# A start ordered by hand up to the guard's branch, and the softmax sums' load two steps earlier

## The chip, the core and the metric

The kernel runs on one core of one Trainium2 chip. The metric is the device time of one execution in microseconds; before the change the median of three runs is 1902.31 us (1900.91 to 1903.0). The engines are TensorE (matmuls and transposes), VectorE, ScalarE, GpSimd and SyncE (SP), which issues most transfers.

## The reference, cut to what matters

One layer norm feeds two branches, whose results are added to the input:

```python
xn = layernorm(x)                                   # x: 2048 x 512
# A: attention, 32 heads of 16, one shared key and value head
p  = softmax(einsum("bhqd,bkd->bhqk", q, k) * 16**-0.5)
A  = einsum("bhqk,bkd->bhqd", p, v) ... @ wo
# B: product-key experts, 4096 experts, per token and head 2 of 64 x 64
s1, s2 = q1 @ k1.T, q2 @ k2.T                       # top 2 of each, top 2 of the 4 sums
g  = softmax(top_s);  act = gelu(xn . u[top_e])
B  = sum(g * act * v[top_e])
return x + A + B
```

In the inputs B has 32 heads with two halves of 128, so its queries' product with the keys is folded into a weight of 512 columns for each chunk of four heads (8 chunks).

## The kernel before, in words

The 2048 rows are 16 tiles of 128, in four groups of four tiles. Numbers that must keep float32 precision are split in a high and a low part, and a product is the sum of three matmuls (high by high, high by low, low by high).

The start (L1213 to L1253) does the following for each group g: load x, norm_group (L145: statistics and normalisation on VectorE, one square root on ScalarE), transpose_group (L171: 16 transposes, a copy on ScalarE and a subtraction on VectorE for each of four 512-wide tiles, a store to DRAM for later groups), project_kv (L194: 12 matmuls for the shared key and value, the key's parts copied by six small transfers into kaug), and project_q (L222: four blocks r of 12 matmuls, a high part on ScalarE, a low part on VectorE, both stored to DRAM; the square of the block is summed by a matmul with blk, for the length of the queries). wq is split into halves first (L1227 to L1232).

The experts' part starts there too. score_thread (L1114) is a generator: wp_make(c) (L482) folds chunk c's weights with four products (pw, from a loaded tile wqT) and four sets of transposes (pwt) with splits; item (L519) then gives one tile's scores for the chunk (12 matmuls psc) and finds the best by max and max_index on VectorE; the fourth item of a chunk ends in batch (L569), which makes indices and gates. Each step yields a cost, which is added to a planned time, spent. run_scores (L1130) drives it to a planned time or to a key. In the start it runs chunk 0 to its end. The gathers (L987) then fetch expert rows by index into up to NGB = 12 buffers, which they share with other tiles of the start.

guard (L251) compares a bound, the longest query by the longest key, with a limit. The flag is loaded by all engines, and the rare branch computes true maxima; with these inputs it isn't taken. In front of this branch the order of the instructions is the framework's planner's. Behind it, an order written by hand holds: each engine's queue has the instructions in the order of the program text.

The loop (L1256 to L1347) has 256 steps d of att_steps (L1159), i = 2d. In a step four score pairs (sc: two 64-row matmuls) go to PSUM, ScalarE takes their exponentials (pt), and the value products (pv) of the step before follow. A unit u is 16 values of i: 512 queries and four heads. In the middle (mid) come VectorE's dots and sums for the gathered experts; at the end fill() runs run_scores up to a planned time, aim, which grows evenly with d. So TensorE is filled with chunk products, and in phases 2 and 3 with a dense form of the experts (dense, L655).

Two units make a pair pp. Its softmax sums go to DRAM at the start of the step with r = i mod 32 = 2 (unit_tail's spread, L351); pair_load (L372) reads them back as 128 x 32 at r = 4, pair_invert (L377) takes reciprocals on VectorE at r = 6 and stores them, pair_spread (L382) reads them broadcast at r = 10, and pair_tail (L387) multiplies. At the start of the step with r = 4, load_q (L308) issues eight transfers for the next unit; SP issues in order, and a transfer's wait blocks what is behind it.

At i = 0 the step loads the maxima rows of the query tile (load_q with rows=False) and runs two steps of wp_make(1) ahead of the first scores (L1167).

Of the kernel before, what the change touches and what calls it, by code (L numbers as in the profile page):

```python
# [11 lines left out]
F32 = mybir.dt.float32  # L12
# [43 lines left out]
def tile_kernel(ctx, tc, x, wq, wkv, wo, wqT, kT, uv, ub, vb, out):  # L56
# [39 lines left out]
    zk(kaug)  # L96
    qa_bufs = []
# [4 lines left out]
    vaug = const.tile([P, NT, 32], F32, name="vaug")  # L102
    nc.gpsimd.memset(vaug, 1.0)
# [15 lines left out]
    ones_f = start.tile([2, 512], F32, name="ones_f")  # L119
    nc.gpsimd.memset(ones_f, 1.0)  # L120
# [6 lines left out]
    XT, XS, XN, ACC, XP = [], {}, {}, {}, [None]  # L127
# [17 lines left out]
    def norm_group(g, xs):  # L145
        mv = start.tile([P, GT, 2], F32, name="mv", bufs=2)
        for j in range(GT):
            st = start.tile([P, 6], F32, name="st", bufs=2)
            nc.vector.bn_stats(st, xs[j])
            nc.vector.bn_aggr(mv[:, j, :], st)  # L150
        v = start.tile([P, GT], F32, name="ve", bufs=2)
        nc.vector.tensor_scalar(v, mv[:, :, 1], 1e-5, None, op0=OP.add)
        sd = start.tile([P, GT], F32, name="sd", bufs=2)
        nc.scalar.activation(sd, v, AF.Sqrt)
# [9 lines left out]
        for j in range(GT):  # L164
            t = g * GT + j
            nc.vector.tensor_scalar(XN[t], xs[j], mv[:, j, 0:1], rs[:, j:j + 1],
                                    op0=OP.subtract, op1=OP.mult)
            if 1 <= g < NSP:
                nc.sync.dma_start(d_xn[t - TPH], XN[t])

    def transpose_group(g):  # L171
        first = g < 1
        XS[g] = []
        for k in range(KC):
# [10 lines left out]
            XS[g].append(xt)  # L185
            if not first:
                nc.sync.dma_start(d_xt[g - 1][k], raw(xt[:]))
# [3 lines left out]
    ksq_p = None  # L191
    qmax = const.tile([P, NGRP], F32, name="qmax")

    def project_kv(g):  # L194
        p = stile("pkv")[:, 0, :]
        n = 0
        for k in range(KC):
            for a, b in TERMS:
                w = (wkv_h, wkv_l)[a]
                nc.tensor.matmul(p[:32, :], w[:, k, :], XS[g][k][:, b, :], start=n == 0, stop=n == 11)  # L200
                n += 1
        kv = big.tile([32, 512], F32, name="kv", tag="wk", bufs=NWK)
        nc.scalar.copy(kv, p[:32, :])
        kh = big.tile([32, 2, 512], F32R, name="kh", tag="wk", bufs=NWK)
        nc.vector.tensor_copy(kh[:, 0, :], kv)
        nc.vector.tensor_tensor(out=kh[:, 1, :], in0=kv, in1=kh[:, 0, :], op=OP.subtract)
        c = slice(g * 512, (g + 1) * 512)
        for base in (0, 64):
            nc.sync.dma_start(raw(kaug[base:base + 16, c]), raw(kh[:16, 0, :]))
            nc.sync.dma_start(raw(kaug[base + 16:base + 32, c]), raw(kh[:16, 1, :]))  # L210
            nc.sync.dma_start(raw(kaug[base + 32:base + 48, c]), raw(kh[:16, 0, :]))
        sq = start.tile([16, 512], BF16, name="ksq", tag="sq", bufs=2)
        nc.vector.tensor_mul(sq, kv[:16, :], kv[:16, :])
        nc.tensor.matmul(ksq_p[32 * g:32 * g + 32, :], blk[:16, 0:1].to_broadcast([16, 32]), sq,
                         start=True, stop=True)
# [6 lines left out]
    def project_q(g, wqs):  # L222
        pq = xtile("pqs")
        for r in range(KC):
            p = stile("pq")[:, 0, :]
            n = 0
            for k in range(KC):
                for a, b in TERMS:
                    nc.tensor.matmul(p, wqs[k][:, a, r * P:(r + 1) * P], XS[g][k][:, b, :],
                                     start=n == 0, stop=n == 11)  # L230
                    n += 1
            q = [start.tile([P, 512], F32R, name="qt", tag="qt", bufs=4) for _ in range(2)]
            nc.scalar.copy(q[0], p)
            nc.vector.tensor_tensor(out=q[1], in0=p, in1=q[0], op=OP.subtract)
            sq = start.tile([P, 512], BF16, name="qsq", tag="sq", bufs=2)
            nc.scalar.activation(sq, p, AF.Square)
            nc.tensor.matmul(pq[32 * r:32 * r + 32, :], blk, sq, start=True, stop=True)
            c = slice(g * 512, (g + 1) * 512)
            nc.sync.dma_start(d_qh[r * P:(r + 1) * P, c], raw(q[0][:]))
            nc.sync.dma_start(d_ql[r * P:(r + 1) * P, c], raw(q[1][:]))  # L240
        nc.vector.reduce_max(qmax[:, g:g + 1], pq, axis=AX.X)
# [9 lines left out]
    def guard():  # L251

        mm = small.tile([P, 2], F32, name="mm", bufs=1)
        nc.vector.reduce_max(mm[:, 0:1], qmax, axis=AX.X)
        nc.vector.reduce_max(mm[:, 1:2], ksq_p, axis=AX.X)
        p = xtile("pm")
        for i in range(2):
            nc.tensor.transpose(p[:1, i * P:(i + 1) * P], mm[:, i:i + 1], ident)
        m2 = small.tile([1, 2], F32, name="m2", bufs=1)
        nc.vector.reduce_max(m2, p[:1, :2 * P].rearrange("p (a n) -> p a n", a=2), axis=AX.X)  # L260
        pr = small.tile([1, 1], F32, name="prd", bufs=1)
        nc.vector.tensor_mul(pr, m2[:, 0:1], m2[:, 1:2])
        fl = small.tile([1, 1], I32, name="flag", bufs=1)
        nc.vector.tensor_scalar(fl, pr, LIMIT2, None, op0=OP.is_gt)
        flag = nc.values_load(fl[0:1, 0:1], min_val=0, max_val=1)
# [205 lines left out]
    def wp_load(c, h):  # L471
        if late[0] is None or (c == 1 and h < 2):
            w = gtile(F32, (P, 2, D), "wqt") if c == 0 and h > 1 else big.tile([P, 2, D], F32, name="wqt", tag="wqt", bufs=2)
        else:
            w = late[0].tile([P, 2, D], F32, name="wqt", tag="gy", bufs=3)
# [6 lines left out]
    def wp_make(c):  # L482
# [13 lines left out]
        for k in range(KC):  # L496
# [7 lines left out]
            store(lambda k=k, wk=wk: nc.sync.dma_start(d_w[c][:, k], raw(wk[:])))  # L504
# [570 lines left out]
    ON_ACT, LATER_ACT, LAST, LATER, BEHIND, STORES, POST, POST_FILL = [], [], [], [], [], [], [], []  # L1075
    store = STORES.append
# [81 lines left out]
    def att_steps(d, mid, fill):  # L1158
# [4 lines left out]
        if i < STEPS:  # L1163
            u, kc = divmod(i, 16)
            if i == 0:
                load_q(0, rows=False)
                run_scores(until=spent[0] + 1.8)  # L1167
# [20 lines left out]
        if pp and pp < 16:  # L1188
            if r == 4:
                pair_load(pp - 1)  # L1190
# [20 lines left out]
    xs = [[load_x(j, True) for j in range(GT)]]  # L1211
    wraws = []
    for i in range(2):  # L1213
        wraw = gtile(F32, (P, 2, 512))
        nc.sync.dma_start(wraw, wq[i * 256:(i + 1) * 256, :].rearrange("(k p) n -> p k n", p=P))
        wraws.append(wraw)
    for h in range(4):
        wp_load(0, h)
    for g in (1, 2):
        xs.append([load_x(g * GT + j, False) for j in range(GT)])  # L1220
    norm_group(0, xs[0])
    transpose_group(0)
    ksq_p = ps.tile([P, 512], F32, name="ksq_p", tag="pv", bufs=1)
    nc.vector.tensor_copy(wkv_h, wkv_f)
    nc.vector.tensor_tensor(out=wkv_l, in0=wkv_f, in1=wkv_h, op=OP.subtract)
    wqs = []
    for i in range(2):  # L1227
        for k in range(2):
            w = start.tile([P, 2, 512], F32R, name="wqs", tag="wqs", bufs=4)
            nc.scalar.copy(w[:, 0, :], wraws[i][:, k, :])  # L1230
            nc.vector.tensor_tensor(out=w[:, 1, :], in0=wraws[i][:, k, :], in1=w[:, 0, :], op=OP.subtract)
            wqs.append(w)  # L1232
    project_kv(0)
    norm_group(1, xs[1])
# [153 lines left out]
```

## Time and profile before

| what | us |
| --- | --- |
| runs, median | 1902.31 |
| profiled execution | 1899.53 |
| its span, first to last instruction | 1897.7 |
| TensorE busy | 1813.9 |
| VectorE busy | 1628.2 |
| ScalarE busy | 1286.8 |
| GpSimd busy | 694.7 |

The mean granted clock of TensorE is 0.991. A row of the timeline has the start, the length, the engine, the line, the operation with its output and inputs, and how many are merged; in brackets stands the idle time before it and what ended it. PEld is the weight load, which runs beside the matmul. A name with a q (SPq, PEq) is an engine's queue or sequencer. Matmuls are pipelined, and their ends in the trace are modelled.

### The profile page before, as it was taken

Reading aid. Unit: us, or ns where it says so; the run is one execution under the profiler, and the core shown is the slowest. Engines: PE = TensorE matmul, PEld = TensorE weight load, DVE = VectorE, ACT = ScalarE, POOL = GpSimd, SP = SyncE. Lnnn points to the kernel's source line nnn. Section 1 sums busy time; section 2 is a strip of 40 time slices with the busy share of each in tenths; the row PEclk is TensorE's granted clock in tenths of the full one; section 3 lists DMA queues with packets and bytes.
Section 4 is the critical chain, followed back from the end, with each engine's and each line's share of the span. In section 5 each row is a group of like instructions: output and inputs, shape, how many; then the busy total and the mean of one; then the engine's idle time right before and its main releaser. Section 6 shows DMA issues by size and latency. Waiting matters only on the chain.

```text
span 1897.7 us, 34925 instructions
## 1 busy us (share of the span) xinstructions
PE 1813.9 (96%) x10990; PEld 956.6 (50%) x10990; DVE 1628.2 (86%) x6381; ACT 1286.8 (68%) x1739; POOL 694.7 (37%) x920
## 2 busy tenths in 40 slices
PE   6979998999999899999999899999998999999998
PEld 3634444555555344555555454555544355555553
DVE  6628888999988977999899797999989778999995
ACT  3346665655557987887777555555579877788874
POOL 1203444434443123344434354344531124444430
PEclk9989999999999999999999999999999999999999
DMA  7857899897773677889899887877735868899883
GB/s 267 317 194 284 304 323 310 294 334 247 235 263 109 222 245 233 258 266 284 266 287 315 321 316 234 267 260 236 254 109 194 271 205 274 287 292 292 277 274 105
DMA packets 243706, 489.75 MB, mean 258 GB/s; under 512 B 93748, under 2 KB 106420, under 8 KB 243516
## 3 DMA queue, kind: packets, MB, share of 16 engines
q0 software_dynamic: 73728, 268.47, 42.4%
q1 hardware_dynamic: 168552, 218.18, 35.1%
q8 instruction: 88, 1.44, 0.3%
q10 hardware_dynamic: 1236, 0.82, 0.1%
q14 instruction: 102, 0.84, 0.1%
HBM read 426.49 MB, written 55.61 MB: 254 GB/s over the span
## 4 chain that ended last, share of the span: by engine, by line
PE 75%; DVE 9%; DMA 4%; ACT 3%; issue 2%; SPq 1%; DVEq 0%; ACTq 0%
PE pv L341 21%; PE psc L536 19%; PE sc L327 15%; PE pact L738 9%; PE pout L876 8%; DVE oh L797 2%; PE pwo L439 2%; ACT pt L330 2%; DVE xa L1043 1%; PE pw L492 1%; DVE g L1008 1%; DMA gy<-dg 1%; DVE oh L800 1%; DMA wqt<-in_wqT_dram 1%; DVE oh L799 1%
## 5 line engine op out<-in xcount | busy, mean ns | idle before, releaser
L330 ACT ACTIVATE pt<-sc 128x1024 f32<-128x1024 f32 x1024 | 994.5, 1028 | 433.8 <-PE sc L327 431.1
L996 POOL DMA_INDIRECT g<-in_uv_dram,idx x512 | 554.7, 1083 | 1013.8 <-DVE xa L1043 508.9
L341 PE MATMUL pv<-pt,vaug 128*32 128x512 f32 x4096 | 494.8, 601 | 0.0
L327 PE MATMUL sc<-qa,kaug 64*128 64x512 f32 x2048 | 387.7, 450 | 20.1 <-ACT pt L330 19.5
L536 PE MATMUL psc<-wk,xt 128*128 128x512 f32 x1536 | 388.2, 400 | 3.8 <-DVE wk L502 3.8
L1043 DVE SCALAR_TENSOR_TENSOR xa<-g,w,xa 128x512 f32<-128x512 f32 x512 | 371.1, 743 | 0.1
L1008 DVE CUSTOM_DVE_ANT_0 g<-g,xa 128x512 f32<-128x512 f32 x512 | 334.5, 679 | 9.5 <-DMA g<-in_uv_dram,idx 9.5
L536 PEld LDWEIGHTS psc<-wk,xt 128*128 128x128 f32 x1536 | 277.9, 188 | 107.1 <-issue 40.4
L327 PEld LDWEIGHTS sc<-qa,kaug 64*128 64x128 f32 x2048 | 156.8, 185 | 337.8 <-ACT pt L330 244.2
L341 PEld LDWEIGHTS pv<-pt,vaug 128*32 128x32 f32 x4096 | 107.1, 109 | 243.5 <-issue 243.5
L876 PE MATMUL pout<-wk,wd 128*128 128x512 f32 x768 | 197.3, 405 | 9.9 <-DVE wd L939 7.0
L551 DVE FIND_INDEX8 i<-m,psc 128x8 uint32<-128x64 f32 x1024 | 206.0, 218 | 0.0
L738 PE MATMUL pact<-xt,wk 128*128 128x512 f32 x768 | 195.9, 400 | 0.0
L876 PEld LDWEIGHTS pout<-wk,wd 128*128 128x128 f32 x768 | 142.0, 190 | 58.5 <-DVE wd L939 8.3
L549 DVE MAX8 m<-psc 128x8 f32<-128x64 f32 x1024 | 145.8, 212 | 24.3 <-PE psc L536 23.2
L738 PEld LDWEIGHTS pact<-xt,wk 128*128 128x128 f32 x768 | 139.4, 188 | 48.5 <-issue 17.5
L703 DVE TENSOR_TENSOR wk<-rw,wk 128x512 fp32r<-128x512 f32 x128 | 84.9, 681 | 8.3 <-ACT wk L702 8.2
L879 DVE TENSOR_TENSOR da<-da,pout 128x512 f32<-128x512 f32 x128 | 82.9, 677 | 9.5 <-PE pout L876 9.2
L797 DVE TENSOR_TENSOR oh<-oh 128x2048 f16<-128x2048 f16 x64 | 78.0, 1218 | 2.7 <-ACT oh L764 2.7
L702 ACT CAST wk<-rw 128x512 fp32r<-128x512 f32 x128 | 74.1, 633 | 0.0
L1031 DVE SCALAR_TENSOR_TENSOR w<-gth,ga 128x4 f32<-128x4 f32 x128 | 20.0, 156 | 57.8 <-ACT gth L1024 57.6
L551 DVE MATCH_VALUE_LOAD i<-m,psc 128x8 f32 x1024 | 68.2, 67 | 0.0
(159 smaller groups left out, 1327.9 us busy)
## 6 DMA issues: line engine op xcount, KB each, us to landing
wk<-dw SPq DMA_DIRECT2D x96, 512.0 KB
wqt<-in_wqT_dram SPq DMA_DIRECT2D x32, 512.0 KB
dw<-wk SPq DMA_DIRECT2D x32, 512.0 KB
rw<-in_ub_dram SPq DMA_DIRECT2D x64, 256.0 KB
rw<-in_vb_dram SPq DMA_DIRECT2D x64, 256.0 KB
gy<-dg SPq DMA_DIRECT2D x64, 256.0 KB
dg<-gst SPq DMA_DIRECT2D x14, 928.0 KB
qa<-dqh SPq DMA_DIRECT2D x128, 64.0 KB
```

Of the source, the lines that this page charges most:

```text
L327: nc.tensor.matmul(p[:, b, :], kaug[o:o + 64, kc * P:(kc + 1) * P], QA[u][o:o + 64, i, :], start=True, stop=True)
L330: nc.scalar.activation(pt, p, AF.Exp, scale=SCALE)
L341: nc.tensor.matmul(PV[u][32 * j:32 * j + 32, :], vaug[:, kc, :], pt[:, b, :], start=kc == 0, stop=kc == 15)
L536: nc.tensor.matmul(p, XT[k][:, a, j * P:(j + 1) * P], WC[n_][k][:, bb, :], start=n == 0, stop=n == 11)
L549: nc.vector.max(m8[:, jb, s, :], p[:, s * E:(s + 1) * E])
L551: nc.vector.max_index(i8[:, jb, s, :], m8[:, jb, s, :], p[:, s * E:(s + 1) * E])
L738: nc.tensor.matmul(p, us[:, a, k * P:(k + 1) * P], XT[k][:, c, :], start=n == 0, stop=n == 11)
L797: nc.vector.tensor_tensor(out=oa, in0=num(P), in1=bc(0, tb, P), op=OP.is_equal)
L876: nc.tensor.matmul(p, wd[0][:, a, j * P:(j + 1) * P], vs[:, c, :], start=n == 0, stop=n == 5)
L996: nc.gpsimd.indirect_dma_start(out=gt, out_offset=None, in_=uv, in_offset=bass.IndirectOffsetOnAxis(ap=IDX[ph, c, ti][:, s:s + 1], axis=0))
L1008: nc.vector.tensor_tensor_reduce(u, u, XN[TPH * ph + ti], scale=1.0, scalar=0.0, op0=OP.mult, op1=OP.add, accum_out=a[:, i:i + 1])
L1043: nc.vector.scalar_tensor_tensor(acc, v, w[:, i:i + 1], acc, op0=OP.mult, op1=OP.add)
```

## The change

- The part in front of the branch is under the hand-written order as well, one engine queue each. Functions are cut in pieces for that: norm_stats and norm_apply; key_products, key_rows, value_rows, key_squares; query_products, query_sq, query_high, query_low, query_squares. The matmul that sums a block's squares is issued behind the next block's products. Products go through the terms with the k blocks inside (FIRST), so that all high parts come first.
- Statistics and applications of a group are issued ahead of the block that needs them; wq's high halves are copied ahead of group 0's application, two low halves behind it and two behind the transposes.
- Stores are collected and issued at given points (STORES, and BULK for the 512 KB ones).
- All four weight tiles of the second chunk are loaded in the start, in four of the shared buffers, and wp_make(1) runs whole in front of the branch: two products ahead of group 3's keys, two behind the last query block around its square, and the four sets of transposes behind the flag's computation. Six gathers in place of twelve are issued in front of the branch.
- The keys' bound goes through kmax, the square of the key and its high part are made on ScalarE; qt has six buffers in place of four, the squares three in place of two. The ones for kaug come from vaug, by SP.
- In the loop: at i = 0 no steps of wp_make ahead of the scores; a GpSimd copy reads the query tile's maxima rows, so GpSimd's gathers wait for them; two weight tiles of chunk 2 are loaded; the bulk stores left over are handed on. The first step has no dots. The planned time starts 5.4 lower than spent, the cost of wp_make(1).
- pair_load comes at r = 2 in place of r = 4.

```diff
-    def project_q(g, wqs):
-        pq = xtile("pqs")
-        for r in range(KC):
...
+    def query_low(g, r, engines=None):
+        q = QT[r % 2]
+        nc.vector.tensor_tensor(out=q[1], in0=PQ[r % 2], in1=q[0], op=OP.subtract)
+        e = engines or nc.sync
+        c = slice(g * 512, (g + 1) * 512)
+        store(lambda: e.dma_start(d_qh[r * P:(r + 1) * P, c], raw(q[0][:])))
+        store(lambda: e.dma_start(d_ql[r * P:(r + 1) * P, c], raw(q[1][:])))
...
             if i == 0:
                 load_q(0, rows=False)
-                run_scores(until=spent[0] + 1.8)
+                nc.gpsimd.tensor_copy(PK["mm"][32:64], raw(QA[0][32:64, 0, 0:1]))
+                wp_load(2, 0)
+                wp_load(2, 1)
+                STORES.extend(BULK)
+                BULK.clear()
...
-            if r == 4:
+            if r == 2:
                 pair_load(pp - 1)
...
+    with tc.manual_schedule(engines=ENGINES):
+        load_group(0)
...
+        load_group(1)
...
+        for h in range(4):
+            wp_load(0, h)
+        load_group(2)
+        for h in range(4):
+            wp_load(1, h)
+        norm_stats(0, range(GT))
...
+        for k in range(KC):
+            nc.scalar.copy(wqs[k][:, 0, :], wraws[k // 2][:, k % 2, :])
+        norm_apply(0)
+        wq_half(0)
+        wq_half(1)
+        transpose_group(0)
+        wq_half(2)
+        wq_half(3)
...
+        def queries(g, r, *between):
+            stores(2)
+            query_products(g, r)
+            query_sq(g, r)
+            for fn in between:
+                fn()
+            query_high(g, r)
+            query_low(g, r)
+
+        key_products(0)
+        queries(0, 0, lambda: norm_stats(1, range(2)), lambda: key_rows(0))
+        queries(0, 1, lambda: value_rows(0), lambda: query_squares(0, 0), lambda: norm_stats(1, range(2, GT)))
+        queries(0, 2, lambda: key_squares(0), lambda: query_squares(0, 1), lambda: norm_apply(1))
+        queries(0, 3, lambda: query_squares(0, 2), lambda: norm_stats(2, range(2)))
+        score_steps(4)
+        norm_stats(2, range(2, GT))
+        query_squares(0, 3)
+        zero_m()
+        transpose_group(1)
+        stores()
+        load_group(3)
+        score_steps(4)
+        stores(4)
+        key_products(1)
...
+        queries(2, 2, lambda: key_squares(2), lambda: query_squares(2, 1))
+        flush()
+        queries(2, 3, lambda: query_squares(2, 2))
+        load_q(0, maxima=False)
+        gathers(NGB // 2)
+        transpose_group(3)
+        query_squares(2, 3)
+        score_steps(2)
+        stores(4)
+        key_products(3)
...
+        query_products(3, 3)
+        query_sq(3, 3)
+        query_high(3, 3)
+        score_steps(1)
+        query_squares(3, 3)
+        score_steps(1)
+        guarded = guard_flag(longest)
+        next(guarded)
+        query_low(3, 3, nc.scalar)
+        fl = next(guarded)
+        stores()
+        assert not BULK
+        score_steps(4)
     start_stack.close()
...
-        done0 = spent[0]
+        done0 = spent[0] - 5.4
...
-            todo = max(min(int(pos + 0.001), g_next[0]) - d_next[0], 0)
+            todo = max(min(int(pos + 0.001), g_next[0]) - d_next[0], 0) if d else 0
```

256 lines of the change are left out of this document (138 added, 118 removed).

## The prediction

> **What bounds the kernel now.** I read the page first.
>
> ```profile
> span 1897.7 us, 34925 instructions
> ...
> PE 1813.9 (96%) x10990; PEld 956.6 (50%) x10990; DVE 1628.2 (86%) x6381; ACT 1286.8 (68%) x1739; POOL 694.7 (37%) x920
> ...
> PE 75%; DVE 9%; DMA 4%; ACT 3%; issue 2%; SPq 1%; DVEq 0%; ACTq 0%
> ```
>
> TensorE is busy for 96% of the span and carries 75% of the chain of waits. A change that leaves its matmuls as they are can gain only from its idle time, 83.8 us in all, and from stretches at a low clock. So the second view is the busy time by window, cut at the events that the change touches: TensorE's second start, the flag, the branch's exit, the first expert-score matmul (psc) behind the branch, and one stall late in the loop.
>
> ```profile
> 0.00:17.45 17.45, 3.67 (x14) 2.53 (x15) 10.37 (x27) 5.21 (x9) 7.89 (x24) 1.00 0.93 321
> 17.45:122.31 104.86, 94.28 (x408) 61.57 (x408) 61.77 (x219) 35.65 (x64) 13.87 (x21) 0.96 0.75 276
> 122.31:127.42 5.11, 0.00 (x0) 0.03 (x1) 0.70 (x3) 0.00 (x0) 0.00 (x0) 0.50 0.03 10
> 127.42:145.92 18.50, 12.88 (x64) 4.67 (x64) 3.58 (x12) 12.92 (x17) 0.00 (x0) 0.88 0.52 172
> 145.92:1897.70 1751.78, 1703.05 (x10504) 887.82 (x10504) 1551.76 (x6122) 1233.07 (x1650) 672.93 (x875) 0.99 0.79 258
> 1051.86:1064.65 12.79, 6.02 (x18) 4.25 (x17) 10.44 (x27) 2.55 (x4) 5.54 (x5) 0.73 1.02 360
> ```
>
> The columns are the stretch, its length, the busy time of TensorE, weight loads, VectorE, ScalarE and GpSimd, the granted clock, the DMA share and GB/s. Ahead of 145.92 TensorE idles for 13.8 + 10.6 + 5.1 + 5.6 = 35.1 us, and some of its busy time runs at half clock. The timeline of TensorE gives the places.
>
> ```profile
> 17.45 0.66 PE L182 MATMUL ptr<-ident,xa 128*128 128x128 f32 x4 [2.27 <-DVE xt L184]
> ...
> 44.31 3.65 PE L492 MATMUL pw<-wqt,kTs 128*64 128x512 f32 x14
> ...
> 75.91 0.38 PE L237 MATMUL pqs<-qsq,blk 128*32 128x512 bf16 x1 [2.53 <-DVE act L1008]
> ...
> 118.20 0.39 PE L237 MATMUL pqs<-qsq,blk 128*32 128x512 bf16 x1
> 120.34 0.38 PE L237 MATMUL pqs<-qsq,blk 128*32 128x512 bf16 x1 [1.75 <-ACT qsq L236]
> 121.69 0.58 PE L258 MATMUL pm<-ident,mm 128*1 128x128 f32 x2 [0.98 <-DVE mm L254]
> 127.42 3.68 PE L492 MATMUL pw<-wqt,kTs 128*64 128x512 f32 x8 [5.15 <-PEq L266]
> ...
> 133.04 0.73 PE L327 MATMUL sc<-qa,kaug 64*128 64x512 f32 x4
> ...
> 140.27 1.92 PE L341 MATMUL pv<-pt,vaug 128*32 128x512 f32 x16
> ...
> 145.92 0.50 PE L536 MATMUL psc<-wk,xt 128*128 128x512 f32 x1 [1.60 <-DVE wk L502]
> ```
>
> **The start, to TensorE at full work.** VectorE shows why TensorE waits at 17.45: it had queued the second group's statistics ahead of the first group's subtractions, and those wait for a transfer.
>
> ```profile
> 3.77 0.69 DVE L149 BATCH_NORM_STATS2 st<-xa 128x6 f32<-128x512 f32 x1 [3.77 <-DMA xa<-in_x_dram]
> ...
> 10.82 1.91 DVE L166 TENSOR_SCALAR xa<-xa,mv,rs 128x512 f32<-128x512 f32 x4
> 12.64 1.29 DVE L1231 TENSOR_TENSOR wqs<-g,wqs 128x512 fp32r<-128x512 f32 x2
> 16.11 0.69 DVE L149 BATCH_NORM_STATS2 st<-xp 128x6 f32<-128x512 f32 x1 [2.18 <-DMA xp<-in_x_dram]
> ```
>
> Two of the four halves of wq had also gone ahead of the applications (the two left are at 12.64). The change puts the four applications first, about 1 us earlier, then two halves (1.3 us), then the subtractions, with nothing of group 1 between. Applications end near 11.8, halves near 13.1, the first subtraction near 13.8, which frees the PSUM tile for the fourth set of transposes; by my count the key products run without a break from 14.25. So at 17.45 twelve key products and a query product are done, where before four transposes (0.5 us) and eleven key products (0.23 us each, 94.28 us for 408) were still to come: **3.0 us** ahead.
>
> **From there to the last query product.** Before it ends at 118.20. Idle from 17.45 to 122.31 is 10.58, of which 1.75 + 0.98 lie behind 118.20: 7.85 in front. The new order lets the square's matmul of one query block follow the next block's products, so that nothing waits for ScalarE, and gives qt six buffers in place of four. What stays are the transposes, whose PSUM tiles VectorE frees.
>
> ```profile
> L184 DVE TENSOR_TENSOR xtt<-ptr,xtt 128x512 fp32r<-128x512 f32 x12 | 8.1, 687 | 4.4 <-ACT xtt L183 4.0
> L183 ACT CAST xtt<-ptr 128x512 fp32r<-128x512 f32 x12 | 6.7, 588 | 8.7 <-PE ptr L182 8.7
> ```
>
> Four transposes take some 0.5 us (0.66 at 17.45 with the last one's tail), a copy 0.59, a subtraction 0.69, with three tiles. I count 0.3 to 0.8 us of stall in each of three groups, and 1 us where the chunk's own four splits follow group 1's: 2.2 us left. Gain **5.6 us**.
>
> The clock:
>
> ```profile
> 77.00:78.00 1.00, 0.76 (x4) 0.20 (x2) 0.95 (x2) 1.00 (x3) 0.93 (x1) 0.60 1.07 393
> 84.00:85.00 1.00, 1.00 (x5) 0.59 (x4) 0.11 (x1) 0.00 (x0) 0.00 (x0) 0.98 1.04 418
> 131.00:132.00 1.00, 0.10 (x2) 0.00 (x0) 0.00 (x0) 0.59 (x1) 0.00 (x0) 0.59 1.05 401
> ```
>
> It is at half from about 77.4 to 84.0, behind the 2.53 us hole at 75.91, with TensorE nearly all busy: half of 6.4 us, **3.2 us**, goes if no such hole is left. [...]
>
> Added in front of that point are the first two weight products of the second chunk, eight matmuls at 3.57/14 = 0.255 us: **+2.0 us**, and one square's matmul that before came later, +0.3. So the last query product ends at 118.2 - 3.0 - 5.6 - 3.2 + 2.3 = 108.7. A bound on the other side: a matmul alone is listed with 0.38 us (120.34), the step is 0.23, so in front of each of about nine holes 0.15 us counts as busy that isn't; that makes 107.3. I take **107.3** (105 to 111).
>
> **The branch.** The flag came 4.9 us behind 118.20; from the flag to TensorE's next work it took 4.3.
>
> ```profile
> 122.94 0.14 DVE L264 TENSOR_SCALAR flag<-prd 1x1 int32<-1x1 f32 x1
> ...
> L266 PEldq COMPARE_BRANCH  x1: 3388/3388/3388, 123.7 to 123.7; - x1
> ```
>
> TensorE's branch instruction alone has 3.39 us. The guard is the same, so this stays. [...] The change puts the second chunk's transposes and splits there: the last two weight products, the flag at +3.6 (4.9 less a copy of 0.59 and a subtraction of 0.69, which now come behind the square), the four sets of transposes, paced by ScalarE, until about +6. TensorE is out at 107.3 + 6 + 4.3 = **117.6** (115.2 with 3.6 in place of 6, if the splits hide; 118.6 with 7, if all engines wait for VectorE's last split).
>
> **Behind the branch.** Before, 18.50 us pass to 145.92, because the weights are loaded there (the first scores come at 133.04) and the copies, the exponentials' table and the splits share ScalarE.
>
> ```profile
> 127.43 0.58 SPq L314 DMA_DIRECT2D qa<-dm  x2
> ...
> 133.75 1.28 ACT L330 ACT_TABLE_LOAD   x1
> 135.05 3.77 ACT L330 ACTIVATE pt<-sc 128x1024 f32<-128x1024 f32 x4
> ```
>
> After, only 16 score and 16 value matmuls are left in front of the same psc. The scores wait for the maxima (qa<-dm). Its landing isn't shown; the first load of x, issued at 0.80 into empty queues, was used at 3.77, so 3.0 us (bounds: 0, and 5.6, since at 133.04 it had landed).
>
> ```profile
> 0.80 1.81 SPq L142 DMA_DIRECT2D xa<-in_x_dram  x4
> ```
>
> The table is loaded in front of the branch now, as the gates' exponential moves behind the last square root. Eight exponentials at 1.03 us (0.94 apart in pairs) with two PSUM tiles: the sixth ends 6.9 us after the first score, the last score follows, psc begins 7.6 after it. So 117.6 + 10.6 = **128.2** against 145.92: **17.7 us** gained, and the planned position in the fill is the same there (two steps of 1.8 before, the same point after). The cold clock can cost more: it came back at 131.6, 4.2 us behind the restart. If scores alone, at a half of TensorE's time, don't bring it back, the sixteen value matmuls (1.85 us) take as long again: 0 to 1.9.
>
> Six fewer gathers stand ready at the branch (six, then four, then two). VectorE's first dots use those six, so I cost this at nothing; without that cover one gather's time is late, about 1 us. Two megabytes more of weights in the first transfers come behind all x but the last group; nothing waits for them before 30. Zero, or 2 us if SP's queue holds up the q stores.
>
> **The sums' chain.** pair_load moves from r = 4 to r = 2, so on SP it goes in front of load_q's eight transfers. Of its 15 uses one shows in the waits:
>
> ```profile
> 1027.26 0.38 SPq L694 DMA_DIRECT2D gy<-dg  x1
> ...
> 1038.34 0.44 SPq L374 DMA_DIRECT2D rc<-dsum  x1
> ...
> 1050.82 0.35 DVE L379 RECIPROCAL rc<-rc 128x32 f32<-128x32 f32 x1 [8.25 <-DMA rc<-dsum]
> ...
> 1055.07 0.96 PE L876 MATMUL pout<-wk,wd 128*128 128x512 f32 x3 [3.21 <-DVE wd L939]
> 1059.59 5.13 PE L876 MATMUL pout<-wk,wd 128*128 128x512 f32 x13 [3.56 <-DVE wd L939]
> ```
>
> The load took 12.5 us with the queues full, VectorE stood for 8.25, TensorE for 6.77, and the clock (0.73 in that window) cost 1.8 more on thirteen matmuls. Moved, the load is issued at about 1027.7, 10.6 earlier; even with the same 12.5 it lands 2.3 us before VectorE asks. Gain **8.3 us** (0 to 8.6). What is late next is the second subtraction into wd: 1059.59 - 8.25 = 1051.3, and TensorE needs it some 0.7 us behind 1051.86.
>
> **Sum.** 1899.53 is the profiled execution, 1.83 over its span; the median of three is 1902.31, 2.78 above it, and I carry that. 1902.31 - 17.7 - 8.3 = **1876.3**.
>
> **Rivals.** (1) *Prologue gains half.* Transfers or SP's order take the place of the planner's holes: before, VectorE stood 5.6 us once for a q store.
>
> ```profile
> L234 DVE TENSOR_TENSOR qt<-pq,qt 128x512 fp32r<-128x512 f32 x16 | 11.0, 687 | 18.9 <-ACT qt L233 12.5 <-DMA dql<-qt 5.6 <-DMA kaug<-kh 0.9
> ```
>
> For: 0.75 DMA share from 17.45 on, more bytes in front. Against: six gathers fewer, six buffers. 1902.3 - 8.85 - 8.3 = 1885.2. (2) *The sum's load is late anyway*, the queues being full, or another wait takes VectorE's place: 1902.3 - 17.7 = 1884.6. (3) *Slower.* At r = 2 SP must wait for d_sum's own landing, with load_q, weights and gates queued behind it, 15 times. Only a pair's four ot transfers and what a step's end stores stand between; a landing with full queues was 12.5 above, so up to that each, 190 in all. It decides above 26.0/15 = 1.7 us lost on the path per pair; at 2.0 the result is 1906. Against: what is queued behind is mostly due many microseconds later, and the full stretches are few. (4) *The order by hand equals the planner's* and the stall stays: 1902.
>
> **Chances.** Forecast 0.66, its own range 1870 to 1882; rival 1 0.12, rival 2 0.11, both at once 0.03 (1893); rival 3 0.05; rival 4 0.03. The range for eight in ten takes in rivals 1 and 2 and the bounds of the branch: 1868 to 1888. A change under 0.2%, 3.8 us, can't be told from none. Faster 0.92, same 0.03, slower 0.05.
>
> **What would show it.** Right: TensorE's first transposes near 10.5 and no hole over 1 us before the last query product at 107; no half clock there; a branch of about 3.4 us on TensorE; only scores, exponentials and value matmuls between the exit near 118 and psc near 128; no table load in the loop; the reciprocal on rc without a wait. Wrong: SP's queue with waits for wqT or qt in the first 100 us, a wait for d_sum ahead of pair_load with load_q late behind it, TensorE still idle near 1050.

## The result and the profile after

| kernel, one chip | median us | runs | range |
| --- | --- | --- | --- |
| before | 1903.67 | 12 | 1900.91 to 1907.65 |
| after | 1892.80 | 12 | 1884.02 to 1899.94 |

The ratio is 0.994, 95% interval 0.9922 to 0.9958. The change is faster, by 10.9 us and not by the 26.0 that the forecast of 1876.3 meant; 1892.8 lies outside the range of 1868 to 1888. The profiled execution of after is the slowest of its twelve (1899.94), so its span says little of the gain: set against the profiled execution of before (1899.53) it gained nothing. The two traces show in which places time was won and lost, and not where the median's 10.9 us come from. From the page of after:

```profile
span 1898.2 us, 34936 instructions
...
PE 1820.5 (96%) x10989; PEld 958.7 (51%) x10989; DVE 1628.7 (86%) x6377; ACT 1287.9 (68%) x1745; POOL 694.1 (37%) x920
...
PE 69%; DVE 11%; DMA 7%; ACT 3%; issue 2%; SPq 1%; POOL 0%; DVEq 0%; ACTq 0%; POOLq 0%
```

TensorE's share of the chain fell from 75% to 69%; transfers rose from 4% to 7%. The windows of after, cut at TensorE's first transpose, the end of the last query product, the end of the flag's computation and the first psc behind the branch:

```profile
0.00:10.15 10.15, 0.00 (x1) 0.04 (x1) 5.79 (x18) 3.04 (x6) 7.40 (x23) 1.00 0.86 284
10.15:115.24 105.09, 97.14 (x429) 65.51 (x429) 68.43 (x232) 40.24 (x76) 7.85 (x15) 0.97 0.81 276
115.24:118.67 3.43, 3.31 (x18) 1.19 (x17) 1.94 (x6) 2.21 (x5) 0.00 (x0) 1.00 0.03 11
118.67:135.59 16.92, 9.88 (x45) 3.78 (x43) 2.58 (x4) 7.96 (x11) 5.82 (x7) 0.70 0.65 208
...
1050.00:1100.00 50.00, 49.06 (x285) 26.08 (x280) 38.65 (x177) 29.94 (x38) 17.25 (x19) 1.00 0.97 356
```

The psc that stood at 145.92 stands at 135.59: 10.3 us gained, where 17.7 were forecast. The last row is the stretch in which the sum's load stalled before, and the stall is gone: TensorE is busy for 49.06 of 50 us, and VectorE's reciprocal on rc starts without a wait (no bracket):

```profile
1049.48 0.35 DVE L422 RECIPROCAL rc<-rc 128x32 f32<-128x32 f32 x1
```

TensorE's timeline gives the places ahead of psc:

```profile
10.15 4.31 PE L189 MATMUL ptr<-ident,xa 128*128 128x128 f32 x16 [10.15 <-DVE xa L174]
14.11 1.61 PE L209 MATMUL pkv<-xt,wkv_h 128*32 128x512 f32 x4
...
106.00 5.15 PE L251 MATMUL pq<-xtt,wqs 128*128 128x512 f32 x12 [4.89 <-DVE qt L267]
...
112.20 3.06 PE L251 MATMUL pq<-xtt,wqs 128*128 128x512 f32 x12
...
126.00 1.42 PE L370 MATMUL sc<-qa,kaug 64*128 64x512 f32 x4 [5.33 <-DMA qa<-dm]
...
131.71 3.29 PE L384 MATMUL pv<-pt,vaug 128*32 128x512 f32 x16
...
135.59 0.73 PE L579 MATMUL psc<-wk,xt 128*128 128x512 f32 x2
```

A hole of 4.89 us stands in front of a query block, and its twelve matmuls then take 5.15 us where the next twelve take 3.06: the granted clock was 0.50 from 106 to 110, behind the hole, and 1.00 from 111. The releaser named is a subtraction on VectorE. What VectorE did before it is the finding of this study:

```profile
95.91 0.69 DVE L1051 CUSTOM_DVE_ANT_0 g<-g,xa 128x512 f32<-128x512 f32 x1 [1.99 <-DMA g<-in_uv_dram,idx]
...
102.19 0.69 DVE L1051 CUSTOM_DVE_ANT_0 g<-g,xa 128x512 f32<-128x512 f32 x1 [1.49 <-DMA g<-in_uv_dram,idx]
...
103.15 0.67 DVE L221 TENSOR_TENSOR kh<-kv,kh 32x512 fp32r<-32x512 f32 x1
104.64 0.69 DVE L1051 CUSTOM_DVE_ANT_0 g<-g,xa 128x512 f32<-128x512 f32 x1 [0.82 <-DMA g<-in_uv_dram,idx]
105.26 0.08 DVE L1051 DVE_READ_ACCUMULATOR2_ANT act<- 128x1 f32 x1
105.26 0.68 DVE L267 TENSOR_TENSOR qt<-pq,qt 128x512 fp32r<-128x512 f32 x1
```

L1051 is the dot of the gathered experts. The program text has it in the loop, behind the branch; the trace has six of them ahead of the flag (118.67) by 14 to 25 us, in VectorE's queue in front of the key's and the query's subtractions. Each dot waits for its gather; together, the six wait 8.5 us:

```profile
DVE g L1051 <- DMA g<-in_uv_dram,idx: 8.5, 6, 2.0
```

So the order written by hand didn't keep the loop's first VectorE instructions behind the branch; all that these read lies in front of it. The kernel before has two such dots (VectorE's timeline of before):

```profile
73.92 0.69 DVE L1008 CUSTOM_DVE_ANT_0 g<-g,xa 128x512 f32<-128x512 f32 x1 [3.70 <-DMA g<-in_uv_dram,idx]
...
75.18 0.69 DVE L1008 CUSTOM_DVE_ANT_0 g<-g,xa 128x512 f32<-128x512 f32 x1
```

Behind the branch a second loss follows in after. SP's queue, then TensorE's:

```profile
126.65 2.55 SPq L547 DMA_DIRECT2D dw<-wk  x4
129.25 1.18 SPq L519 DMA_DIRECT2D wqt<-in_wqT_dram  x1
130.48 0.93 SPq L357 DMA_DIRECT2D qa<-dm  x1
...
146.60 0.30 SPq L362 DMA_DIRECT2D qa<-dql  x1
147.00 3.23 SPq L519 DMA_DIRECT2D wqt<-in_wqT_dram  x3
```

```profile
155.84 1.98 PE L535 MATMUL pw<-wqt,kTs 128*64 128x512 f32 x4 [4.43 <-DMA wqt<-in_wqT_dram]
...
190.09 1.98 PE L535 MATMUL pw<-wqt,kTs 128*64 128x512 f32 x4 [3.15 <-DMA wqt<-in_wqT_dram]
```

Eight q loads for the second unit stand in front of the fourth weight tile of the third chunk, and with full queues (share 1.02 to 1.04 from 133 to 157) they took SP from 130.48 to 146.9. The tile's buffer was free from 138.2 (three buffers, and the product at 137.17 had read the first); SP issued the load at 147.00. TensorE then waits twice, 7.6 us, each time with half the clock behind it (0.50 granted from 155.8 to 161 and from 190.1 to 195; 1.98 us for four matmuls, 1.08 elsewhere). The second wait is for a tile of the next chunk, which SP issued at 178.94, behind four stores; that it too goes back to the q loads is seen only from the runs below in which these come late, and both waits are gone.

A way to follow the time through a run is the start of the n-th of the 1024 exponentials, in one profile less that in another. After less before: -10.3 us at the 9th, +2.1 at the 33rd, so 12.4 us are lost between 139 and 195; then +6.3 at the 345th and -1.7 at the 537th: 8.0 gained at the sum's load. The 4.2 us between the 33rd and the 345th aren't followed up; two profiles of before differ by more there, as the next section says.

### The profile page after: what moved, and what is told of

Its sections match the earlier page's. It is cut to its first block, busy times and chain, and to the rows that moved or that the text cites. A ratio compares the mean times of both kernels' runs of the same rounds, so it can differ in the third digit from the quotient of the medians.

```text
span 1898.2 us, 34936 instructions
## 1 busy us (share of the span) xinstructions
PE 1820.5 (96%) x10989; PEld 958.7 (51%) x10989; DVE 1628.7 (86%) x6377; ACT 1287.9 (68%) x1745; POOL 694.1 (37%) x920
## 4 chain that ended last, share of the span: by engine, by line
PE 69%; DVE 11%; DMA 7%; ACT 3%; issue 2%; SPq 1%; POOL 0%; DVEq 0%; ACTq 0%; POOLq 0%
PE pv L384 19%; PE psc L579 17%; PE sc L370 13%; PE pact L781 8%; PE pout L919 8%; ACT pt L373 2%; DVE xa L1086 2%; PE pwo L482 2%; DVE oh L840 2%; DMA wqt<-in_wqT_dram 2%; DVE g L1051 2%; DMA gy<-dg 1%; PE pw L535 1%; DMA dinv<-rc 1%; DMA g<-in_uv_dram,idx 1%
## 5 line engine op out<-in xcount | busy, mean ns | idle before, releaser
L1051 DVE CUSTOM_DVE_ANT_0 g<-g,xa 128x512 f32<-128x512 f32 x512 | 335.4, 681 | 14.8 <-DMA g<-in_uv_dram,idx 14.8
```

The costliest lines, as they stand in the source:

```text
L1051: nc.vector.tensor_tensor_reduce(u, u, XN[TPH * ph + ti], scale=1.0, scalar=0.0, op0=OP.mult, op1=OP.add, accum_out=a[:, i:i + 1])
```

## The experiments

The kernel before took 1903.7 us on the chip of the result and 1912 to 1916 on the others, so every ratio is to the kernel before on the same chip, in the same batch.

Before was profiled once more, on another chip (one execution, 1916.47 us). There its first exponential starts at 140.08 and not at 135.05, and 12.3 us more are lost between the 33rd and the 345th. So the profile that the forecast was worked out from has a faster start than this one, and a difference between two single profiles on different chips holds several microseconds that no edit made. One stretch is steadier: from the 9th to the 33rd exponential each of the two profiles of before takes 43.3 us, and the profiles of changed kernels in which no product waits for wqT there take 43.3 to 44.4. After takes 55.7, in its repeats below 49.7 and 49.5, and with the sum's load at r = 4 it takes 53.8: the loss behind the branch is 6 to 12 us.

**The sum's load, undone and alone.** In after, and alone in before:

```diff
-            if r == 2:
+            if r == 4:
                 pair_load(pp - 1)
```


> The changed kernel with pair_load back at r = 4. If the stall of VectorE near 1050 us (8.25 us before the change, gone after it) is worth what stands in the trace, this is 8 us slower than the changed kernel: 1892.8 + 8 = 1901, and its trace has the wait for rc again. If the loop makes that time good elsewhere, it is within 2 us of 1892.8.

```diff
-            if r == 4:
+            if r == 2:
                 pair_load(pp - 1)
```


> The kernel before with pair_load at r = 2 and nothing else. Theory of the sum: 1903.7 - 8.3 = 1895.4. Rival (a pair's load waits for its own sums and holds SP's queue): no gain, 1903 or more. If it is near 1895, the start ordered by hand has brought only about 2.5 us in all.

Measured: after with r = 4 has ratio 0.9956 (0.9941 to 0.9971), before with r = 2 0.9946 (0.9924 to 0.9969), some 10 us of 1914.1. VectorE's row in after with r = 4, and in before with r = 2:

```profile
1058.44 0.35 DVE L422 RECIPROCAL rc<-rc 128x32 f32<-128x32 f32 x1 [7.79 <-DMA rc<-dsum]
```

```profile
1056.62 0.35 DVE L379 RECIPROCAL rc<-rc 128x32 f32<-128x32 f32 x1
```

The wait is there with the one and not with the other. Between the 313th and the 537th exponential, the stretch that holds it, the second kernel gains 8.7 us on the first profile of before; a repeat of after gains 6.9 on the second profile of before, in which the reciprocal waits 5.88 us (481st to 537th exponential, same chip). So this part is worth about what was forecast (8.3), and the start as changed, by the first of the two ratios, only some 8 us. After itself wasn't run on this chip, so the 8 us that undoing the load was to cost aren't measured as such: its ratios elsewhere, 0.990 to 0.994, put that at 0.2 to 0.6%.

**Dots held behind the branch.** A VectorE copy that reads the maxima rows, loaded first thing in the loop, is put in front of the loop's dots in VectorE's queue, to hold them:

```diff
                 nc.gpsimd.tensor_copy(PK["mm"][32:64], raw(QA[0][32:64, 0, 0:1]))
+                nc.vector.tensor_copy(PK["mm"][96:128], raw(QA[0][96:128, 0, 0:1]))
```


> The changed kernel with one more small VectorE copy at i = 0 that reads the maxima rows, so that no dot of the loop's first steps can be placed in front of the branch. In the trace after, six such dots wait 7.0 us in all for gathers there, and TensorE has a hole of 4.9 us and half a clock behind it. Theory A: the hole goes, the last query product ends near 108 instead of 115.2, and psc behind the branch comes 7 us earlier; but the loads of wqT and the six late gathers then start earlier into the same full queues, so most of the 7 is given back by 200 us only if the transfers set the time there: 1886 if it is kept, 1891 if not. Rival: the dots are merely moved behind the branch and cost there what they cost before it: 1892 to 1894.

Measured: 1887.54 us, ratio 0.9857 (0.9831 to 0.9882). (The 7.0 us of the expectation leave out the first of the six dots.) The copy waits 4.1 us for its load, and no dot is among VectorE's seven longest waits from 60 to 125 us, where after's six come first with 8.5 us. TensorE's timeline:

```profile
101.28 3.07 PE L251 MATMUL pq<-xtt,wqs 128*128 128x512 f32 x12
...
108.40 1.08 PE L535 MATMUL pw<-wqt,kTs 128*64 128x512 f32 x4
...
119.25 1.42 PE L370 MATMUL sc<-qa,kaug 64*128 64x512 f32 x4 [5.37 <-DMA qa<-dm]
...
128.58 1.66 PE L579 MATMUL psc<-wk,xt 128*128 128x512 f32 x6
```

The hole and the half clock are gone (1.00 granted from 60 to 107), and psc begins at 128.58; the prediction said 128.2. So the dots are the cause of the loss ahead of the branch. The loss behind it stays: two waits of 2.2 us at the weight products, and 50.9 us from the 9th to the 33rd exponential, 7.6 more than in before.

**Which bytes.** First, six more gathers ahead of the branch, as before had them, with dots held:

```diff
         score_steps(4)
+        gathers(NGB // 2)
```


> The same with six more gathers issued in front of the branch, right behind the flag, so that twelve are under way there as before the change. Theory B: in the loop's first 70 us TensorE waits 7.6 us for wqT and stands at half clock behind each wait, because six gathers (3 MB), four stores of the second chunk (2 MB) and the loads of wqT share the queues at the loop's start; with the gathers ahead the waits near 151 and 187 us go, and this is 10 to 13 us faster than without them: 1875 to 1880. Rival C: SP's order (stores and query rows in front of wqT) sets it, whatever the gathers do: waits stay, and the time is within 3 us of the run without them.

Measured: 1887.67 us, ratio 0.9863 (0.9842 to 0.9884), no difference, where 10 to 13 us were expected. Its waits on TensorE:

```profile
PE sc L370 <- DMA qa<-dm: 8.0, 1, 8.0
PE pq L251 <- ACT kv L212: 3.3, 1, 3.3
```

Here nothing waits for wqT and nothing is lost behind the 9th exponential. But ahead of it a copy on ScalarE comes late (3.3 us, and the next twelve matmuls take 5.49), and the maxima too (8.0 for 5.4). Four of the six gathers went out by 98; the last two waited for buffers to 115. So by this profile about as much is lost, in another place. That the gathers' bytes cause it there isn't shown: the trace doesn't name what the copy waits for, and one of four profiles of the kernel with held dots has no wait for wqT either.

Then, on another chip, after again, dots held again, and with the latter the 512 KB stores handed on at i = 6:

```diff
+            if i == 6:
                 STORES.extend(BULK)
                 BULK.clear()
```


> The changed kernel as it is, on the chip of this group. Ratio to before 0.994 as measured first (0.9922 to 0.9958). If the parts add, it lies at 0.9956 x 0.9946 = 0.990, from the run with the load at r = 4 and the one with that edit alone; if the start's gain is lost whatever the load does, at 0.994 to 0.995.

> The changed kernel with the dots held behind the branch, again, beside the changed kernel on one chip. The theory that the dots in front of the branch cost the start its gain: 0.986 again, and 7 to 14 us under the changed kernel; its exponentials stand 14 to 17 us ahead of before at the loop's start, and lose 5 to 10 of that in the first 70 us of the loop. If 0.986 was luck of the chip: within 4 us of the changed kernel.

> The same with the dots held, and the four stores of the second chunk's weights (2 MB) handed on at i = 6 in place of i = 0. Rival C (what stands in front of wqT on SP and in the queues delays it, above all these stores): the waits for wqT near 145 and 178 shrink and the loss of the loop's first 70 us with them: 3 to 6 us faster than with the dots held alone. Theory B (all transfers of that stretch together fill the queues, the order matters little): within 2 us.

Measured: after 0.9898 (0.9874 to 0.9923), dots held 0.9835 (0.9807 to 0.9864), with late stores 0.9835 (0.9807 to 0.9863). Neither of the last two profiles shows a wait for wqT, so this pair decides nothing on the weights. On one chip, then, the held dots bring 13.8 us, 0.6%; by the profiles 6.0 of this stand at the 9th exponential, and 6.4 come up to the 33rd, where after waits for wqT and the profile with held dots doesn't.

Next three edits of one line, the first in before (two dots held), the other two on top of the held dots:

```diff
                 load_q(0, rows=False)
+                fence = small.tile([P, 1], F32, name="fence", bufs=1)
+                nc.vector.tensor_copy(fence[96:128], raw(QA[0][96:128, 0, 0:1]))
```


> The kernel before, with nothing changed but that its own two dots, which stood in VectorE's queue in front of the guard's branch, are held behind it. Theory (the dots that wait for gathers cost both kernels): its 2.53 us hole at 75.9 and most of the half clock behind it (3.2 us) go, so some 4 to 6 us faster, ratio .997 to .998, and the first exponential starts that much earlier. Rival (in the kernel before the hole was the query sums' own, and only the new order is hurt by dots): the hole stays under another name, ratio 1.000 within .001.

```diff
-                    gathers(4)
+                    gathers(4 if d > 2 else 0)
```


> The changed kernel with dots held, and the six gathers (3 MB) that follow the branch are put behind the loop's first two steps in GpSimd's order. Theory B (the gathers share the queues with the weights of the loop's first units): where the kernel with dots held waits for wqT, here it doesn't, and the loss between the 8th and 32nd exponential (7.6 us on the first chip) falls to under 3, so 2 to 6 us faster than that kernel; where that kernel has no such waits on this chip, nothing. Rival C (SyncE's own order, eight loads of q and four stores of dw in front of the weights): waits and time unchanged within .1%. A third: the dots then come late, VectorE has them to do beside the sums of later units, and 1 to 3 us are lost.

```diff
-            if kc == 4 and u + 1 < 32:
+            if kc == (4 if u else 10) and u + 1 < 32:
                 load_q(u + 1)
```


> The changed kernel with dots held, and the second unit's eight q loads issued at the first unit's key block 10 instead of 4, so that the weights of the loop's first units stand in front of them in SyncE's order. Rival C (SyncE's order delays wqT): the waits for wqT go where the kernel with dots held has them, and 2 to 6 us with them. Theory B (the bytes of the gathers): waits and time unchanged within .1%. If the second unit's own work starts before its q is there, a wait for q appears in its place and it is 1 to 3 us slower.

> The changed kernel with the loop's dots held behind the branch, unchanged from the earlier run of it; here it is the reference for the two kernels that differ from it in one line. Expected as before: ratio to the kernel before .983 to .986. Whether the first products of the loop wait for wqT on this chip (2.2 us twice on one chip so far, not on another) is read from its trace, and decides how much the next two can show.

Measured: dots held 0.9859 (0.9839 to 0.9879), 1890.38 us; late gathers 0.9878 (0.9860 to 0.9897), 1893.63; late q 0.9838 (0.9818 to 0.9859), 1884.89; before with its two dots held 0.9994 (0.9978 to 1.0011).

*Before with held dots* is the rival's case. The dots are gone from the start, and a hole of 4.37 us stands there all the same (TensorE's timeline, then SP's):

```profile
79.98 0.58 PE L237 MATMUL pqs<-qsq,blk 128*32 128x512 bf16 x1 [4.37 <-issue]
```

```profile
75.88 4.61 SPq L187 DMA_DIRECT2D dxt<-xtt  x2
```

VectorE and ScalarE both stand in it, and the trace names no releaser; two stores of the transposed x are being issued for 4.61 us with full queues (from 74 to 84 us a DMA share of 1.00 to 1.03, 371 to 412 GB/s). That these are the cause wasn't tried. The second profile of before, with its dots in place, has the hole at 77.66, 3.18 us long, and there too no releaser is named. In before, then, the dots only stood where something else was late too.

*Late gathers* did not do what it says. GpSimd's queue with held dots alone, and with the edit:

```profile
119.90 1.37 POOL L1039 DMA_INDIRECT g<-in_uv_dram,idx  x1 [0.50 <-DMA qa<-dm]
...
126.54 0.94 POOL L1039 DMA_INDIRECT g<-in_uv_dram,idx  x1 [0.30 <-issue]
```

```profile
119.53 1.28 POOL L1039 DMA_INDIRECT g<-in_uv_dram,idx  x1 [0.50 <-POOL mm L1209]
...
126.09 0.94 POOL L1039 DMA_INDIRECT g<-in_uv_dram,idx  x1 [0.30 <-issue]
```

GpSimd's queue has nothing but gathers there, so a later place in the text is no later time: the six go out as before, and only later ones are put off; it is 3.2 us slower by the medians, with overlapping intervals. Its profile has no wait for wqT, but loses the time again by the 57th exponential. The bytes of the gathers remain untried behind the branch, except by the ten gathers ahead of it above; they are a rival that these runs leave open beside SP's order.

*Late q* takes the waits for wqT away and is 5.5 us faster than held dots on this chip; the two intervals overlap, and the four cells below repeat it.

**Two causes or one.** Four cells on one chip: after, late q alone, dots held, both (no new edits).

> The changed kernel, unchanged, as the first of four cells on one chip: ratio to the kernel before .990 to .995.

> The changed kernel with the dots where the change left them and only the second unit's q loads issued at key block 10. Theory (two causes that add): its two waits for wqT (4.43 and 3.15 us in the profile of the changed kernel) and the half clock behind them go, so 4 to 9 us faster than the changed kernel, ratio between the two .995 to .998, while the 5 us hole in the query products stays. Rival (one cause: the late start of the loop alone puts the weights late): the waits stay and the time is the same within .1%.

> The changed kernel with the dots held behind the branch: ratio .983 to .986 to the kernel before.

> Both mended. If the causes add: 4 to 6 us faster than the kernel with dots held where that one shows waits for wqT, ratio .981 to .984 to the kernel before; its profile shows neither the 5 us hole in the query products nor a wait for wqT. If there is one cause: the same as the kernel with dots held, within .1%.

| | median us | ratio to before (95%) | n-th exponential against after: 1st, 57th |
| --- | --- | --- | --- |
| after | 1900.47 | 0.9922 (0.9893 to 0.9952) | 0, 0 |
| late q | 1888.96 | 0.9869 (0.9843 to 0.9895) | -0.5, -6.8 |
| dots held | 1891.54 | 0.9875 (0.9846 to 0.9905) | -7.4, -4.9 |
| both | 1885.44 | 0.9847 (0.9819 to 0.9874) | -8.1, -14.5 |

Late q alone leaves the hole and takes away the waits (TensorE's waits, with late q; then TensorE's and SP's timeline with dots held alone; then SP's with both):

```profile
PE pq L251 <- DVE qt L267: 4.5, 1, 4.5
```

```profile
149.96 1.41 PE L535 MATMUL pw<-wqt,kTs 128*64 128x512 f32 x4 [4.23 <-DMA wqt<-in_wqT_dram]
...
181.92 1.08 PE L535 MATMUL pw<-wqt,kTs 128*64 128x512 f32 x4 [2.10 <-DMA wqt<-in_wqT_dram]
```

```profile
123.77 0.61 SPq L357 DMA_DIRECT2D qa<-dm  x1
...
141.72 0.30 SPq L362 DMA_DIRECT2D qa<-dql  x1
142.12 2.42 SPq L519 DMA_DIRECT2D wqt<-in_wqT_dram  x3
```

```profile
122.68 20.36 SPq L519 DMA_DIRECT2D wqt<-in_wqT_dram  x4
```

The last row merges four loads, which start at 122.68, 131.10, 136.88 and 142.67. The second of them is the one for which TensorE waits with dots held alone: SP issues it at 131.10 with both, as soon as its buffer is free, and at 142.12 with dots held. With both no product waits. So there are two causes, and each is there without the other. By the 57th exponential the pair brings more (14.5) than the two alone (6.8 + 4.9), as held dots alone give 2.5 of their 7.4 us back at the waits for wqT. Late q alone brings more than the 4 to 9 us expected: 6.8 of its 11.5 us are there by the 57th exponential, and the rest comes later in the run and isn't located. At the end the pair brings less than the sum: 15.0 us against 11.5 and 8.9. Hence a last pair, on one more chip:

> The changed kernel with late q loads, dots not held, against the next kernel on one chip. If holding the dots is kept to the end, this one is 5 to 8 us slower than the next (the 7.7 us that lie between them at the first exponentials); if it is given back, the two are within 2 us. Ratio to the kernel before .984 to .989.

> Both mended. Ratio to the kernel before .983 to .985. If the gain of the held dots is given back later, its lead over the kernel with late q alone shrinks from some 7 us at the 57th exponential to under 2 at the end, and the trace shows in which stretch; if it is kept, 5 to 8 us stay.

Measured: late q 1885.45 us, 0.9860 (0.9834 to 0.9886); both 1882.92 us, 0.9846 (0.9821 to 0.9870). The lead from the held dots is 7.0 us at the 1st exponential, 5.1 at the 57th, 3.4 at the 465th, 0.6 at the 481st, and -1.3 at the last. In the four cells it goes 7.6, 7.7, 5.8, 3.1 and -0.1. One step is alike in both pairs, 2.7 to 2.8 us between the 465th and the 481st. VectorE's waits from 915 to 950 us, both mended, then late q alone (last pair):

```profile
DVE gy L962 <- DMA gy<-dg: 5.8, 2, 5.3
```

```profile
DVE gy L962 <- DMA gy<-dg: 1.3, 1, 1.3
```

A load of gates lands later relative to its use in the kernel that is ahead, and TensorE waits for VectorE there (1.3 + 1.2 us, none in the other). In the last pair 1.9 us go by the 57th exponential: with both, one weight product waits 1.8 us for wqT at 209.26, the only such wait in five profiles with late q. The rest of what is given back shows no step common to both pairs. So the held dots are worth 8.9 us to the change as it stands (13.8 on the chip where both were first run together); on top of late q, 3.5 and 2.5 us by the medians, which the intervals don't tell from nothing.

Both mended is the fastest version: 0.9838, 0.9847 and 0.9846 on three occasions, against 0.990 to 0.994 for the change alone.

## Why the prediction was wrong, point by point

- **Start, 3.0 us: right.** The first transposes come at 10.15 (about 10.5 forecast), and key products run from 14.11 without a break.
- **To the last query product, 107.3: wrong, and the step that failed is "no hole over 1 us before the last query product at 107".** The end came at 115.24. The hole of 4.89 and about 2.1 of half clock (5.15 less 3.06) are what separates it from 108.4 with held dots, which lies inside 105 to 111. Matmuls, the stalls at the transposes and the added work came out within 1.1 us; what stood in VectorE's queue was read from the program text. The row at 75.91 that the prediction quoted named act, a dot's result, as releaser, in a stretch where the text has no dot. It was quoted and put down to the planner's order, and how a dot came there wasn't asked. Held back in before, the dots bring nothing, as shown above; but they announce the six that stand in after's queue.
- **Branch and what follows: right in sum.** The flag came 3.43 behind the last query product (3.6 forecast), TensorE's branch took 3.85 us (3.39 in before), the other engines' 0.05 to 0.07, which the traces don't explain, and psc began 20.35 us behind the last query product (20.9 forecast). Of its parts, the scores came earlier (10.8 for 13.3) and the exponentials and values took longer (9.6 for 7.6): sixteen value matmuls took 3.29 us for 1.92 (0.50 granted from 131 to 134), inside the bound of 0 to 1.9. Held dots put psc at 128.58.
- **Six fewer gathers, "I cost this at nothing": wrong, and the second step that failed.** The cover named was that VectorE needs only six. What was left out were the queues: 3 MB more of transfers in the stretch where the loop's first weights are loaded, and SP's order, in which eight q loads stand ahead of those weights. That order is the same in before, where SP issued the q loads from 147.6 to 153.2 and the weights by 160.6, with a DMA share of 0.78 from 143 to 151 and 0.71 from 151 to 159; TensorE waited 0.4 us for weights there. The sum took the run behind psc as unchanged. Between the 9th and the 33rd exponential after loses 12.4 us in the profile of the result and 6.2 on the chip where late q alone takes the loss away and brings 11.5 in all. So SP's order is enough to explain it; whether fewer bytes in that stretch would take it away as well stays open.
- **The sum's load, 8.3: right,** 6.9 to 8.7 by the profiles, 10 by the medians of before with r = 2 alone.
- **Rivals.** Rival 1 had the mechanism (transfers and SP's order take the place of the holes) and looked for it ahead of the branch; it was behind. Its half of the prologue, 8.85, is near the 10.3 measured at psc, but the dots did that: the nearness is luck. Rival 2 is out by the row on rc. Rival 3 is out: SP issued the read of the sum 1.5 us behind what stood in front of it (1028.35 against 1026.88), and before with r = 2 gains.

Taken together: 16.5 us were missing. On the chip of the four cells, mending both causes brings 15.0, and the ratio with both, 0.9838 to 0.9847, is at the forecast's 0.9863 (1876.3 by 1902.31) or a little under. That is no proof of the sum's size: both mended wasn't run on the chip of the result, where before is 8 to 12 us faster than on the others, and its medians, 1882.9 to 1885.4 us, are still above 1876.3.

## What to carry to other kernels

Read each engine's queue from the trace and not from the program text, above all at a branch: when a row names a releaser that the text has elsewhere, follow it before anything is counted. When work is taken out from in front of a stretch, list what each queue then issues in that stretch, in order, and ask which of it is needed first: here six gathers (3 MB) moved to where the loop's first weights are loaded, and the eight q loads in front of the fourth weight tile kept SP from 130.48 to 146.9. Check at a few points of the run that a gain at the start is still there: the held dots' lead over late q alone was 7.0 us at the 1st exponential and -1.3 at the last.

## What the runs showed of the hardware

- The granted clock fell to half behind shorter holes than the 2.53 us that the prediction quotes, and not always at once. In the first run with dots held, two holes of 2.2 us at weight products show both (two rows of TensorE's timeline, then the windows behind the first; the clock is the first number behind the last engine's):

```profile
146.61 1.08 PE L535 MATMUL pw<-wqt,kTs 128*64 128x512 f32 x4 [2.22 <-DVE i L594]
...
178.66 1.98 PE L535 MATMUL pw<-wqt,kTs 128*64 128x512 f32 x4 [2.18 <-DMA wqt<-in_wqT_dram]
```

```profile
147.00:148.00 1.00, 1.00 (x6) 0.38 (x4) 0.77 (x3) 0.27 (x1) 0.00 (x0) 0.86 1.01 393
148.00:149.00 1.00, 1.00 (x8) 0.26 (x10) 0.00 (x0) 0.86 (x2) 0.00 (x0) 0.50 0.97 363
```

  Behind the first hole four matmuls ran at full speed before the clock fell; behind the second they took 1.98 us. Behind the hole of 2.10 us at 181.92, quoted above, the clock stayed at 1.00. In after, half clock (0.50) lasted some 6 us behind each of the two waits (155.8 to 161.8, 190.1 to 195.9), and the two waits, 7.6 us, go with 12.4 us lost by the exponentials: some 6 for each.
- The same program differed from execution to execution in its waits at the weight products: the kernel with held dots had 4.4, 0, 4.0 and 6.3 us there in four profiles, two of them on one chip, of which 2.2, 0, 1.2 and 6.3 name the load of wqT as the releaser and the rest VectorE. On the chip of the result after's runs spread by 15.9 us and before's by 6.7; on the other chips before's spread by 10 to 16 as well, so the wider spread isn't a mark of the change.
- The same kernel before had medians from 1903.7 to 1916.1 us on the chips used.
